# Loading order, DMA queues and weight conversion of the first batch in an FFT-mixing and MLP kernel

## Chip, cores, metric

One core of one Trainium2 chip. The metric is the device time of one execution in microseconds (us), as the median of several runs.

## The reference

```python
# x (8, 3008, 256) f32; filt_r, filt_i (1505, 256) f32
# w_in (256, 2048), w_out (2048, 256), both float64
X = np.fft.rfft(x, axis=1)
y = np.fft.irfft(X * (filt_r + 1j * filt_i)[None], n=3008, axis=1).astype(np.float32)
t = y.reshape(8 * 3008, 256)
h = t @ w_in
out = ((h * np.clip(h + 3.0, 0.0, 6.0) / 6.0) @ w_out).astype(np.float32)
```

## The kernel before

A transform of length 3008 = 47 x 64 is done as two stages of matmuls. The first goes over 64 points (`a_unit`, products `psf<-xc,wa`), the second over 47 (`b_unit`), then come the products with the filter on VectorE, the way back (`bi_unit`) and a last stage (`n_unit`, `psn`) that leaves the tokens as the MLP takes them. Between the stages the data goes through DRAM: `z_tmp` (stored by `z_store`, loaded as `t` by `t2_load`) and `g_tmp` (`g_store`, `t4_load`). While the MLP works on batch b, the transform of batch b + 1 is woven into its slots, so only batch 0 has its way to the MLP in the open. The MLP's first product is `psh`.

The weights come as float64 bits (`bits`) and are rounded to float32 on chip, in 16 pieces (`w_conv`). The filter tiles `ft` hold each frequency row twice: rows k2 + 64 s in ascending order and rows 64 j - k2 in descending order. The second kind is the "mirrored" load: 23 partitions, each fetching eight 1 KB rows backwards.

```python
def f_load(c):
    t = ft[c]
    nc.vector.memset(t, 0.0)
    lo = 1 if c == 0 else 0
    for src, p0 in ((filt_r, 0), (filt_i, HALF)):
        nc.gpsimd.dma_start(t[p0:p0 + H, :, :]..., raw(src, c * KC, [[64 * D, H], [1, KC * D]]))   # H = 24
        nc.gpsimd.dma_start(t[p0 + 32:p0 + 32 + H - 1, lo:KC, :],                                   # mirrored
                            raw(src, 64 - c * KC - lo, [[64 * D, H - 1], [-D, KC - lo], [1, D]]))
        # [cut: for c == 0 also row 32 + 64 s]

def b_unit(b, i):
    # [cut: two matmuls into ps from wb and t2]
    nc.vector.tensor_tensor(out=s1, in0=ps, in1=f, op=ALU.mult)
    nc.vector.tensor_tensor(out=s2[0:HALF], in0=ps[0:HALF], in1=f[HALF:P], op=ALU.mult)
    nc.vector.tensor_tensor(out=s2[HALF:P], in0=ps[HALF:P], in1=f[0:HALF], op=ALU.mult)

def up(b, m, jt):
    # [cut: psh = w_in x xn on TensorE]
    r = rp.tile([P, 512], FP32, name="r", tag="r")      # rp: 2 buffers
    g = gp.tile([P, 512], FP32, name="g", tag="g")      # gp: 4 buffers, shared with w_conv's temporaries
    # [cut: r = relu(psh / 6 + 0.5) on ScalarE, g = min(r, 1) * psh on VectorE]

# start of the program
nc.sync.dma_start(wa, wa_d)
for c in range(3): x_load(0, c)                  # SP's queue
for c in range(4): f_load(c)                     # GpSimd's queue
w_load(0); w_load(1)                             # GpSimd's queue
for c in range(6):
    a_unit(0, 2 * c); a_unit(0, 2 * c + 1)
    z_store(0, c)                                # GpSimd's queue
    w_conv(c); w_load(c + 2)
    # [cut: next x_load, or table_load on SP's queue]
# [cut: t2 loads, last tables]
for i in range(17):
    if i < 16:
        b_unit(0, i)
        w_conv(6 + i); w_load(8 + i)             # those past the 16th do nothing
        # [cut: t2 load]
    if i:
        bi_unit(0, i - 1)
        # [cut: g_store after every second unit, GpSimd's queue]
# [cut: t4 loads, n_unit; then the MLP with the next batch in its slots]
```

## Time and profile before

| | before |
|---|---|
| device time, median of 3 | 3359.38 us (3359.05 to 3360.88) |
| span of the profiled execution | 3356.7 us |
| second stage of batch 0 starts | 114.7 us |
| first `psh` (MLP begins) | 237.1 us |
| from first `psh` to the end | 3119.6 us, TensorE full up to its last matmul, 11.9 us before the end |

### The profile page before, as it was taken

To read this page: it belongs to the slowest core of one execution; us is meant where nothing else is said; L and a number is where in the kernel's file an instruction comes from. 1 tells how busy PE (TensorE), PEld (TensorE's weight loads), DVE (VectorE), ACT (ScalarE), POOL (GpSimd) and SP (SyncE) were. 2 spreads that over 40 slices of the span, in tenths; PEclk is the share of its full clock that TensorE was granted. 3 is DMA by queue.
4 is the path that set the end of the run, shared out by engine and by line. 5 is a ranking of instruction groups with operands and counts; after the bars stand their busy time and mean duration, and the time that the engine had idled before them with its cause. 6 is when DMAs were issued, how large, how long until landed. Compare 5 with 4: busy or idle time off the path is not lost.

```text
span 3356.7 us, 28371 instructions
## 1 busy us (share of the span) xinstructions
PE 3203.8 (95%) x11712; PEld 2117.0 (63%) x11712; DVE 919.8 (27%) x1413; ACT 740.8 (22%) x1137; POOL 218.2 (6%) x390
## 2 busy tenths in 40 slices
PE   1469999999999999999999999999999999999998
PEld 0246666666666676666675666666666666666665
DVE  2951232113321233112331133212332123311211
ACT  0012222222222222222222222222222222222221
POOL 2101000010001000010000100000000100000000
PEclk6579999999999999999999999999999999999999
DMA  8432121121212211021211212111111211010000
GB/s 149 140 100 77 32 60 39 37 58 47 55 29 62 52 45 44 24 74 47 65 28 44 62 37 63 32 55 46 52 44 29 74 43 43 24 36 19 19 7 12
DMA packets 76352, 168.20 MB, mean 50 GB/s; under 512 B 17410, under 2 KB 42244, under 8 KB 76032
## 3 DMA queue, kind: packets, MB, share of 16 engines
q0 software_dynamic: 32416, 86.55, 9.7%
q1 hardware_dynamic: 43808, 79.85, 9.2%
q8 instruction: 92, 1.51, 0.2%
q14 instruction: 36, 0.29, 0.0%
HBM read 91.29 MB, written 74.97 MB: 50 GB/s over the span
## 4 chain that ended last, share of the span: by engine, by line
PE 93%; DVE 3%; DMA 2%; issue 1%; POOL 0%; ACT 0%; SPq 0%; POOLq 0%; ACTq 0%
PE po L329 40%; PE psh L312 39%; PE psf L275 6%; PE psf L258 3%; PE psn L300 3%; PE psf L236 2%; DMA ft<-in_filt_i_dram 1%; DMA ft<-in_filt_r_dram 1%; DMA bits<-in_moe_w_in_dram 0%; DVE s L266 0%; DVE s L264 0%; DVE s L265 0%; DVE rest L213 0%; DVE rest L216 0%; DVE big L210 0%
## 5 line engine op out<-in xcount | busy, mean ns | idle before, releaser
L329 PE MATMUL po<-w_out,g 128*128 128x256 f32 (+1 forms) x6144 | 1471.9, 380 | 0.0
L312 PE MATMUL psh<-xn,w_in 128*128 128x512 f32 (+1 forms) x3072 | 1428.5, 587 | 0.0
L329 PEld LDWEIGHTS po<-w_out,g 128*128 128x128 f32 (+1 forms) x6144 | 1138.8, 188 | 398.9 <-issue 271.9
L317 DVE SCALAR_TENSOR_TENSOR g<-r,psh 128x512 f32<-128x512 f32 (+1 forms) x768 | 519.5, 676 | 2301.1 <-ACT r L316 2301.1
L316 ACT ACTIVATE r<-psh,half_c 128x512 f32<-128x512 f32 (+1 forms) x768 | 520.8, 678 | 2210.8 <-PE psh L312 2210.8
L312 PEld LDWEIGHTS psh<-xn,w_in 128*128 128x128 f32 x3072 | 573.8, 190 | 433.7 <-issue 399.2
L275 PE MATMUL psf<-s,wi 128*96 128x256 f32 x1024 | 261.6, 401 | 28.6 <-DVE s L266 28.1
L275 PEld LDWEIGHTS psf<-s,wi 128*96 128x96 f32 x1024 | 174.7, 173 | 131.9 <-issue 49.5
L236 PE MATMUL psf<-xc,wa 128*128 128x512 f32 x192 | 105.3, 639 | 76.2 <-ACT t L237 69.8
L258 PE MATMUL psf<-t,wb 96*128 96x256 f32 x512 | 139.3, 396 | 27.6 <-issue 19.0
L258 PEld LDWEIGHTS psf<-t,wb 96*128 96x128 f32 x512 | 98.5, 197 | 92.7 <-issue 67.5
L345 POOL DMA_DIRECT2D out_dram<-o x96 | 50.9, 535 | 1483.6 <-issue 1443.8
L300 PEld LDWEIGHTS psn<-wai,t 128*128 128x128 f32 x768 | 102.0, 194 | 52.6 <-issue 52.6
L280 ACT ACTIVATE t<-psf 96x512 f32<-96x512 f32 x128 | 75.9, 593 | 235.0 <-PE psf L275 235.0
L247 POOL DMA_DIRECT2D z_tmp<-t x192 | 93.4, 493 | 441.0 <-ACT t L237 414.9
L283 POOL DMA_DIRECT2D g_tmp<-t x64 | 44.6, 698 | 1069.6 <-ACT t L280 1068.6
L236 PEld LDWEIGHTS psf<-xc,wa 128*128 128x128 f32 x192 | 36.8, 203 | 117.8 <-ACT t L237 77.9
L300 PE MATMUL psn<-wai,t 128*128 128x128 f32 x768 | 102.6, 277 | 8.7 <-DMA t<-g_tmp 8.7
L264 DVE TENSOR_TENSOR s<-psf,ft 128x512 f32<-128x512 f32 x128 | 87.7, 685 | 15.2 <-PE psf L258 15.0
L266 DVE TENSOR_TENSOR s<-psf,ft 64x512 f32<-64x512 f32 x128 | 88.9, 695 | 1.8
L265 DVE TENSOR_TENSOR s<-psf,ft 64x512 f32<-64x512 f32 x128 | 87.4, 683 | 3.3
L237 ACT ACTIVATE t<-psf 128x512 f32<-128x512 f32 x96 | 56.9, 597 | 106.4 <-DMA z_tmp<-t 81.4
(34 smaller groups left out, 267.6 us busy)
## 6 DMA issues: line engine op xcount, KB each, us to landing
z_tmp<-t POOLq DMA_DIRECT2D x192, 128.0 KB, 3.6
t<-z_tmp SPq DMA_DIRECT2D x64, 384.0 KB, 3.9
g_tmp<-t POOLq DMA_DIRECT2D x64, 384.0 KB, 3.4
t<-g_tmp SPq DMA_DIRECT2D x192, 128.0 KB, 4.0
xc<-in_x_dram SPq DMA_DIRECT2D x88, 256.0 KB, 4.9
out_dram<-o POOLq DMA_DIRECT2D x88, 256.0 KB, 3.1
bits<-in_moe_w_in_dram POOLq DMA_DIRECT2D x8, 512.0 KB, 4.3
bits<-in_moe_w_out_dram POOLq DMA_DIRECT2D x8, 512.0 KB, 5.2
```

What stands on the lines that cost most here:

```text
L236: nc.tensor.matmul(ps, wa, st["x", b, c][:, 2 * r:2 * r + 2, :], start=True, stop=True)
L247: nc.gpsimd.dma_start(z_d[b, :, r0:r0 + XC, :], t[p0:p0 + 32, :, :])
L258: nc.tensor.matmul(ps[:, u, :], wb[k // KC][:, k % KC, :], st["t2", b, k // TC][:, k % TC, :], start=True, stop=True)
L264: nc.vector.tensor_tensor(out=s1, in0=ps, in1=f, op=ALU.mult)
L265: nc.vector.tensor_tensor(out=s2[0:HALF], in0=ps[0:HALF], in1=f[HALF:P], op=ALU.mult)
L266: nc.vector.tensor_tensor(out=s2[HALF:P], in0=ps[HALF:P], in1=f[0:HALF], op=ALU.mult)
L275: nc.tensor.matmul(ps[0:KR, u, :], wi[k // KC][:, k % KC, q, :], ss[q][:, u, :], start=(q == 0), stop=(q == 1))
L300: nc.tensor.matmul(ps[:, ts(q, P)], st["t4", b, m][:, q, ts(dh, P)], wai, start=True, stop=True)
L312: nc.tensor.matmul(ps[:, 0:w], w_in[:, dt, ts(jt, P)], xn[:, dt, 0:w], start=(dt == 0), stop=(dt == 1))
L316: nc.scalar.activation(out=r[:, 0:w], in_=ps[:, 0:w], func=AXT.Relu, bias=half_c, scale=1.0 / 6.0)
L317: nc.vector.scalar_tensor_tensor(out=g[:, 0:w], in0=r[:, 0:w], scalar=1.0, in1=ps[:, 0:w], op0=ALU.min, op1=ALU.mult)
L329: nc.tensor.matmul(po[q // 2][0:n, q % 2, :], g[:, ds(q * P, n)], w_out[:, jt, :], start=(jt == 0 and q % 2 == 0), stop=(jt == JT - 1 and ...
```

## The change

Its intent: x first; z stores and g stores of batch 0 on ScalarE's queue; filters and tables on SP's queue in the order in which the second stage uses them; t2 loads and weights on GpSimd's queue. The weight conversion falls from twelve VectorE instructions to nine and one multiply on GpSimd, with temporaries in a pool of their own (`cv`); a piece of `w_in` is now 256 columns of both its halves instead of 512 of one. Three conversions lie in the first stage, eight in the second (one for every second unit), and five move into the first five slots of the MLP.

```diff
+    cv = pool("cv", 4)
 def f_load(c):
-        nc.vector.memset(t, 0.0)                       # now once at the start
-            nc.gpsimd.dma_start(...)                   # ascending and mirrored
+            nc.sync.dma_start(...)
 def w_conv(i):
-        e, big, man, sgn = (gp.tile([P, 512], I32, name=n, tag="g") for n in ("e", "big", "man", "sgn"))
-        rest = rp.tile([P, 512], I32, name="rest", tag="r")
-        # [cut: 6 tensor_scalar, 3 scalar_tensor_tensor, 3 tensor_tensor on VectorE]
+        big = cv.tile([P, 512], I32, name="big", tag="cv")
+        rest = cv.tile([P, 512], I32, name="rest", tag="cv")
+        # [cut: 6 tensor_scalar, 1 tensor_tensor, 2 scalar_tensor_tensor on VectorE]
+        nc.gpsimd.tensor_tensor(out=w_part(i)[1], in0=two(rest), in1=two(hi.bitcast(FP32)), op=ALU.mult)
 # start of the program
-        for c in range(4): f_load(c)
         w_load(0); w_load(1)
         for c in range(6):
             # a_unit x 2
-            z_store(0, c)
-            w_conv(c); w_load(c + 2)
+            z_store(0, c, nc.scalar)
+            # next x_load
+            if c % 2: convert(1)                       # w_conv and the next w_load
+        for c in range(4):
+            f_load(c); table_load(c)                   # SP's queue
-        for c in range(3): t2_load(0, c)
+        for c in range(3): t2_load(0, c, nc.gpsimd)
         for i in range(17):
             # b_unit(0, i)
-                w_conv(6 + i); w_load(8 + i)
+                if i % 2 == 0: convert(1)
             # bi_unit(0, i - 1)
-                    g_store(0, i // 2 - 1)
+                    g_store(0, i // 2 - 1, nc.scalar)
+        for i in range(NCONV - done):                  # 5 are left
+            at(i, convert, 1)                          # slots 0 to 4 of the MLP
```

More of the change, by code (lines that the diff above doesn't have):

```diff
@@ L154, in f_load @@
         t = ft[c]
-        nc.vector.memset(t, 0.0)
         lo = 1 if c == 0 else 0
         for src, p0 in ((filt_r, 0), (filt_i, HALF)):
-            nc.gpsimd.dma_start(t[p0:p0 + H, :, :].rearrange("p a d -> p (a d)"),
+            nc.sync.dma_start(t[p0:p0 + H, :, :].rearrange("p a d -> p (a d)"),
                                 raw(src, c * KC, [[64 * D, H], [1, KC * D]]))
-            nc.gpsimd.dma_start(t[p0 + 32:p0 + 32 + H - 1, lo:KC, :],
+            nc.sync.dma_start(t[p0 + 32:p0 + 32 + H - 1, lo:KC, :],
                                 raw(src, 64 - c * KC - lo, [[64 * D, H - 1], [-D, KC - lo], [1, D]]))
             if c == 0:
-                nc.gpsimd.dma_start(t[p0 + 32:p0 + 32 + H, 0, :], raw(src, 32, [[64 * D, H], [1, D]]))
+                nc.sync.dma_start(t[p0 + 32:p0 + 32 + H, 0, :], raw(src, 32, [[64 * D, H], [1, D]]))
     def table_load(c):
@@ L174, in w_part @@
     def w_part(i):
+        p = i // 2
         if i % 2 == 0:
-            i //= 2
-            cols, dt = ts(i // 2, 512), i % 2
-            return moe_w_in[ts(dt, P), cols].bitcast(I32), w_in[:, dt, cols]
-        i //= 2
-        rows = moe_w_out[ts(i, 2 * P), :].bitcast(I32)
-        return rows.rearrange("(a p) d -> p a d", p=P), w_out[:, ts(i, 2), :].rearrange("p a d -> p (a d)")
+            cols = ts(p, 256)
+            src = moe_w_in[:, cols].bitcast(I32)
+            return src.rearrange("(a p) d -> p a d", p=P), w_in[:, :, cols]
+        src = moe_w_out[ts(p, 2 * P), :].bitcast(I32)
+        return src.rearrange("(a p) d -> p a d", p=P), w_out[:, ts(p, 2), :]
     def w_load(i):
@@ L186, in w_load @@
         t = op.tile([P, 1024], I32, name="bits", tag="o")
-        src = w_part(i)[0]
-        nc.gpsimd.dma_start(t if i % 2 == 0 else t.rearrange("p (a d) -> p a d", a=2), src)
+        nc.gpsimd.dma_start(t.rearrange("p (a d) -> p a d", a=2), w_part(i)[0])
         st["bits", i] = t
@@ L195, in w_conv @@
         lo, hi = words[:, :, 0], words[:, :, 1]
-        e, big, man, sgn = (gp.tile([P, 512], I32, name=n, tag="g") for n in ("e", "big", "man", "sgn"))
-        rest = rp.tile([P, 512], I32, name="rest", tag="r")
+        big = cv.tile([P, 512], I32, name="big", tag="cv")
+        rest = cv.tile([P, 512], I32, name="rest", tag="cv")
         v = nc.vector
-        v.tensor_scalar(out=e, in0=hi, scalar1=20, scalar2=0x7FF,
-                        op0=ALU.logical_shift_right, op1=ALU.bitwise_and)
@@ L201, in w_conv @@
-        v.tensor_scalar(out=e, in0=e, scalar1=1151.0, scalar2=896.0, op0=ALU.min, op1=ALU.subtract)
-        v.tensor_scalar(out=big, in0=e, scalar1=0.0, scalar2=None, op0=ALU.max)
-        v.tensor_scalar(out=e, in0=e, scalar1=20.0, scalar2=0.0, op0=ALU.subtract, op1=ALU.max)
-        v.tensor_scalar(out=man, in0=hi, scalar1=0xFFFFF, scalar2=3,
-                        op0=ALU.bitwise_and, op1=ALU.logical_shift_left)
-        v.tensor_scalar(out=sgn, in0=hi, scalar1=31, scalar2=31,
-                        op0=ALU.logical_shift_right, op1=ALU.logical_shift_left)
@@ L208, in w_conv @@
-        v.scalar_tensor_tensor(out=big, in0=big, scalar=23, in1=man,
-                               op0=ALU.logical_shift_left, op1=ALU.bitwise_or)
-        v.tensor_tensor(out=big, in0=big, in1=sgn, op=ALU.bitwise_or)
-        v.scalar_tensor_tensor(out=e, in0=e, scalar=23, in1=sgn,
-                               op0=ALU.logical_shift_left, op1=ALU.bitwise_or)
-        v.scalar_tensor_tensor(out=rest, in0=lo, scalar=9, in1=e,
-                               op0=ALU.logical_shift_right, op1=ALU.bitwise_or)
@@ L215, in w_conv @@
-        rest = rest.bitcast(FP32)
-        v.tensor_tensor(out=rest, in0=rest, in1=e.bitcast(FP32), op=ALU.subtract)
-        v.tensor_tensor(out=w_part(i)[1], in0=big.bitcast(FP32), in1=rest, op=ALU.add)
+        v.tensor_scalar(out=big, in0=hi, scalar1=3, scalar2=0x3FFFFFFF,
+                        op0=ALU.logical_shift_left, op1=ALU.bitwise_and)
+        v.tensor_scalar(out=rest, in0=hi, scalar1=30, scalar2=30,
+                        op0=ALU.logical_shift_right, op1=ALU.logical_shift_left)
@@ new lines, in w_conv @@
+        v.tensor_tensor(out=big, in0=rest, in1=big, op=ALU.bitwise_or)
+        v.tensor_scalar(out=hi, in0=hi, scalar1=20, scalar2=0x7FF,
+                        op0=ALU.logical_shift_right, op1=ALU.bitwise_and)
+        v.tensor_scalar(out=hi.bitcast(FP32), in0=hi, scalar1=897.0, scalar2=None, op0=ALU.is_ge)
+        v.tensor_scalar(out=rest, in0=big, scalar1=23, scalar2=23,
+                        op0=ALU.logical_shift_right, op1=ALU.logical_shift_left)
+        v.tensor_scalar(out=lo, in0=lo, scalar1=9, scalar2=0x3F800000,
+                        op0=ALU.logical_shift_right, op1=ALU.bitwise_or)
@@ L220, in x_load @@
+        rest, big = rest.bitcast(FP32), big.bitcast(FP32)
+        v.scalar_tensor_tensor(out=rest, in0=lo.bitcast(FP32), scalar=1.0, in1=rest,
+                               op0=ALU.subtract, op1=ALU.mult)
+        v.scalar_tensor_tensor(out=rest, in0=rest, scalar=2.0 ** -20, in1=big, op0=ALU.mult, op1=ALU.add)
+        two = lambda t: t.rearrange("p (a d) -> p a d", a=2)
+        nc.gpsimd.tensor_tensor(out=w_part(i)[1], in0=two(rest), in1=two(hi.bitcast(FP32)), op=ALU.mult)
     def x_load(b, c):
@@ L239, in a_unit, with z_store @@
             st.pop(("x", b, c))
-    def z_store(b, c):
+    def z_store(b, c, q=None):
+        q = q or nc.gpsimd
         t = st.pop(("t1", b, c))
@@ L246, in z_store, with t2_load @@
                 r0 = ri * SL + h * H + c * XC
-                nc.gpsimd.dma_start(z_d[b, :, r0:r0 + XC, :], t[p0:p0 + 32, :, :])
-    def t2_load(b, c):
+                q.dma_start(z_d[b, :, r0:r0 + XC, :], t[p0:p0 + 32, :, :])
+    def t2_load(b, c, q=None):
+        q = q or nc.sync
         t = t2p.tile([KR, TC, D], FP32, name="t2")
-        nc.sync.dma_start(t, z_d[b, ts(c, TC), :, :].rearrange("k p d -> p k d"))
+        q.dma_start(t, z_d[b, ts(c, TC), :, :].rearrange("k p d -> p k d"))
         st["t2", b, c] = t
@@ L280, in bi_unit, with g_store @@
         nc.scalar.activation(out=st["t3", b, c][:, r:r + 2, :], in_=ps[0:KR], func=AXT.Copy)
-    def g_store(b, c):
-        nc.gpsimd.dma_start(g_d[b, ts(c, TC), :, :].rearrange("k p d -> p k d"), st.pop(("t3", b, c)))
+    def g_store(b, c, q=None):
+        q = q or nc.gpsimd
+        q.dma_start(g_d[b, ts(c, TC), :, :].rearrange("k p d -> p k d"), st.pop(("t3", b, c)))
     def t4_load(b, m):
@@ L357, with convert @@
             x_load(0, c)
-        for c in range(K2 // KC):
-            f_load(c)
         w_load(0)
         w_load(1)
+        for c in range(K2 // KC):
+            nc.vector.memset(ft[c], 0.0)
+        done = 0
+        def convert(n):
+            nonlocal done
+            for _ in range(n):
+                w_conv(done)
+                w_load(done + 2)
+                done += 1
         for c in range(NB):
@@ L364 @@
             a_unit(0, 2 * c + 1)
-            z_store(0, c)
-            w_conv(c)
-            w_load(c + 2)
+            z_store(0, c, nc.scalar)
             if c + 3 < NB:
                 x_load(0, c + 3)
-            else:
-                table_load(c - 3)
+            if c % 2:
+                convert(1)
+        for c in range(K2 // KC):
+            f_load(c)
+            table_load(c)
+        nc.sync.dma_start(wai, wai_d)
         for c in range(3):
-            t2_load(0, c)
-        table_load(3)
-        nc.sync.dma_start(wai, wai_d)
+            t2_load(0, c, nc.gpsimd)
         for i in range(K2 // 2 + 1):
@@ L378 @@
                 b_unit(0, i)
-                w_conv(NB + i)
-                w_load(NB + i + 2)
                 if i % 2 and i // 2 + 3 < K2 // TC:
-                    t2_load(0, i // 2 + 3)
+                    t2_load(0, i // 2 + 3, nc.gpsimd)
+                if i % 2 == 0:
+                    convert(1)
             if i:
```

## The prediction

> **What bounds the kernel now.** The page comes first: where in the span is TensorE not full? One digit is a fortieth, 84 us.
>
> ```profile
> PE   1469999999999999999999999999999999999998
> DVE  2951232113321233112331133212332123311211
> DMA  8432121121212211021211212111111211010000
> ```
>
> TensorE is full from the fourth slice on, so only the first 240 us or so have time to give. The view by 20 us windows (columns: PE, PEld, DVE, ACT, POOL busy, TensorE's granted clock, DMA share, GB/s) splits them:
>
> ```profile
> 20.00:40.00 20.00, 0.00 (x0) 0.00 (x0) 0.00 (x0) 0.00 (x0) 3.82 (x3) 0.50 1.07 213
> 60.00:80.00 20.00, 3.64 (x4) 1.18 (x4) 6.65 (x13) 1.08 (x2) 3.46 (x7) 0.51 0.49 104
> 120.00:140.00 20.00, 13.09 (x31) 7.36 (x29) 19.30 (x36) 1.19 (x2) 1.25 (x2) 0.59 0.44 132
> 240.00:260.00 20.00, 20.00 (x70) 12.30 (x69) 4.35 (x7) 6.10 (x10) 1.98 (x4) 1.00 0.25 69
> ```
>
> Nothing computes from 20 to 40 us while the DMA engines are full; VectorE is the full one from 120 us; from 240 us it is TensorE. The chain that ended last (start, length, what) names the owners:
>
> ```profile
> 4.02 25.56 DMA ft<-in_filt_r_dram
> 29.86 26.00 DMA ft<-in_filt_i_dram
> ...
> 57.99 15.09 DMA bits<-in_moe_w_in_dram
> ...
> 225.97 3.41 DMA g_tmp<-t
> 230.72 2.84 DMA t<-g_tmp
> 233.76 3.47 PE psn L300 x16
> 237.24 1.81 PE psh L312 x4
> ```
>
> Filters and weights go ahead of the first z stores in GpSimd's queue; ScalarE, the first stage's eviction, therefore sits still (waits, us in total, times, longest):
>
> ```profile
> ACT t L237 <- DMA z_tmp<-t: 81.4, 4, 62.6
> ```
>
> The second stage (16 units of batch 0) starts at 114.7. VectorE's timeline shows what paces it:
>
> ```profile
> 118.18 0.69 DVE L266 TENSOR_TENSOR s<-psf,ft 64x512 f32<-64x512 f32 x1
> 118.90 0.43 DVE L199 TENSOR_SCALAR e<-bits 128x512 int32<-128x512 int32 x1
> ...
> 124.80 0.69 DVE L217 TENSOR_TENSOR w_in<-big,rest 128x512 f32<-128x512 f32 x1
> 125.50 0.69 DVE L264 TENSOR_TENSOR s<-psf,ft 128x512 f32<-128x512 f32 x1
> ```
>
> From one unit's first multiply to the next is 8.72 us (116.78 to 125.50): 2.1 us of products and 6.6 us for the twelve instructions of one conversion. Ten units carry a conversion (16, less the 6 of the first stage); the other six run at 3.36 us (L264 at 214.13 and 217.49). The MLP proper begins at 237.1 (first psh) and then needs 3356.7 - 237.1 = 3119.6 us of full TensorE, which the change barely touches. So the question is: when does the first psh come?
>
> **What the Trainium skill says.** (1) "DMA: Bandwidth & Descriptors", section "Why a DMA increments its semaphore by 16 and not by 1": a transfer is split over the largest k up to 16 that divides the slowest dimension of both sides; 127 partitions give 1. Half the filter loads have 23 rows (the mirrored, descending ones), a prime: k = 1, and on SP's and ScalarE's queues it is always the lowest-numbered engine. The trace agrees for k = 1: among the single packet records the mirrored loads are 356 packets of 4 KB, the first load's beginning one when the last has ended, about 182 ns apart when undisturbed, never more than three running for long. So today, from GpSimd's queue, up to three loads run beside each other on different engines. (2) "GPSIMD Engine Reference", 3.1: a two-input tensor_tensor costs about 2.6 cycles per element. From the page I estimate 512 x 2.6 / 1.2 GHz = 1.1 us for the multiply that goes there; no run here shows it yet. (3) "SBUF — State Buffer", "Who interferes with whom": a VectorE instruction with at most one SBUF input does not contend with GpSimd. The products (PSUM and ft) are such; they follow each conversion, so the multiply hides beside them.
>
> **The change part by part.**
>
> *First stage.* x is first on SP, z stores go to ScalarE's queue. First matmul at about 5 to 6 us (6.22 now). Each of 6 chunks costs ScalarE two evictions of 0.60 us and four DMA issues of about 0.45 us (SP's issues now: three in 1.37 us), 3.0 us, and waits for the landing of the z store two chunks back (4.0 us to landing). That gives 3.3 us a chunk: acts at about 7, 12, 16, 19, 22.6, 26, last issue at 29, landed near 34. Now this is after 110.
>
> *Filters and tables.* They now follow z: the built order shows the first ft loads waiting for completion lanes that the last z stores used last. From 34 us SP's queue sends per filter chunk c two 8 KB-row loads (24 rows: 12 engines), two mirrored loads (k = 1) and the two tables. Engine 0 then carries, in KB: mirrored 2 x 161 + 6 x 184 = 1426; its shares of the rest, 4 x (32 + 24 + 48) + 4 = 420. Beside it from the other queues: t2 8 x 24, g stores 5 x 24, weights 6 x 32 = 504. At 48 ns per KB for the mirrored ones (the 1 KB packets of t<-z_tmp take 46 ns and follow each other at 46 to 50) and 182 / 4 = 45.5 for the rest: 68 + 42 = 110 us. All filters and tables are there at F = 34 + 110 = 144. The chunks come at about 59, 86, 115 and 144.
>
> *Second stage.* Conversion: six tensor_scalar (0.34 when independent, 0.46 when the next one reads the result, as in today's spacing), one tensor_tensor and two scalar_tensor_tensor at about 0.72: 4.5 us in place of 6.6, and 8 of them instead of 10. Alone that would make a pair of units 2 x 2.1 + 4.5 = 8.7 us of VectorE, at best 9.7 with TensorE's turns, so 16 units take 78 us. But four units need 28 us of filter transfer against 19 of work: VectorE is not the bound, engine 0 is. Also, g stores sit in ScalarE's queue and share eight completion lanes with SP: the built order has the second g store waiting for the lane of a mirrored load of chunk 2, the fourth for one of chunk 3. Evictions behind it stop. This keeps units 8 to 11 back, yet not beyond F. After F come units 12 to 15: 1 us for the first matmul, 4 x 2.1 + 2 x 4.5 = 17.4 on VectorE, about 4 for the last product and eviction: last eviction F + 22.5. From the last eviction (225.1) to the first psh it is 12 us now; the way (store, load, psn) stays. First psh: 144 + 34.5 = 178.5, a gain of 58.6.
>
> *First MLP block.* Five conversions move into slots 0 to 4. VectorE then needs 4.5 + 0.7 = 5.2 us a slot against about 3.9 of TensorE (1.72 + 1.73, and 0.86 for a first-stage unit in every second slot), 6.6 us over five slots. Psh has two buffers and the down product lags by two slots, which takes up some; the GpSimd multiply blocks the next conversion's start for about half a microsecond. Loss: 5 us.
>
> Sum: 3359.4 - 58.6 + 5 = 3305.8. Engine 0 may overlap packets of two rings (the 1.07 above is a sum of packet times over 1), so a little less: 3303.
>
> **The rivals.**
> - *The mirrored loads do not pile up on one engine from SP* (spread, or rotating as today). Then chunk 0 is there near 50, VectorE and TensorE pace 78 us, last eviction at about 130, first psh at 142: gain 95 - 5, time 3269. Against it: k = 1 shows in today's packets and the instruction is the same; for it: every HWDGE transfer in this trace divides by 16, so none shows the lowest-engine rule.
> - *Engine 0 is slower than I take it.* Today's mirrored packets take 250 to 400 ns under the tables' traffic, though that includes the wait for other packets that I count separately. At 60 ns per KB for the mirrored ones F becomes 34 + 86 + 42 = 162, the time by the same sum 3324.
> - *Filters are hidden anyway, conversion was the bound* (the change's own intent): the first rival's 3269, since the new VectorE work is what remains.
> - *The MLP's first block loses more*: if VectorE sets all five slots and GpSimd blocks it fully, 10 us instead of 5: 3308.
>
> **Range and chances.** Four in five for the one-engine story, 3303 give or take 12; one in five for about 3270. Faster by over 2% means below 3292.2. That gives 0.31 faster, 0.68 within 2%, 0.01 slower; range 3267 to 3325.
>
> **What would show it.** Mirrored ft loads landing one after the other, 8 to 14 us apart, until about 144; second-stage units in four groups with idle TensorE and VectorE between; ScalarE waiting long with a g store in its queue; the first psh near 178; VectorE full over the first 25 us of the MLP. Wrong would be: units at an even 9 to 10 us a pair from 50 us on with VectorE full (first rival), a first stage that ends after 45, or POOL multiplies well over 1.1 us that VectorE waits for.

## The result

3308.51 us (3308.25 to 3309.39, four runs) against 3359.22 us (3357.64 to 3360.88). The ratio is 0.9849, with a 95% interval of 0.9835 to 0.9863: 1.5% less time, within the 2% that was given 0.68, and 5.5 us from the 3303 on record. Ratios here are the mean time of one kernel's fast runs over that of the other's of the same rounds, so not quite the ratio of the medians quoted.

**Where the time came from.** The strips of the page after the change, a fortieth (83 us) per digit:

```profile
PE   3589999999999999999999999999999999999998
DVE  4642332123311332113321233212332123312211
DMA  6442110211112121121211112122110211010000
```

TensorE is near full from the third slice on instead of the fourth. The chain of waits that ended last, start, length and what, gives the story of batch 0:

```profile
30.93 17.79 DMA ft<-in_filt_i_dram
...
53.03 4.73 DMA z_tmp<-t
58.05 8.43 DMA t<-z_tmp
66.58 2.06 PE psf L260 x4
71.66 27.35 DMA ft<-in_filt_r_dram
100.16 2.09 PE psf L260 x4
106.69 16.08 SPq L158
123.11 21.22 DMA wb<-wb_t
144.47 2.06 PE psf L260 x4
...
178.36 2.62 PE psh L315 x4
```

The second stage does not wait for VectorE any more. It waits for filters and tables, again and again: 27 us for a filter load, 16 us in SP's sequencer (SPq), 21 us for a table behind the filters. The 27 us reach the stage by a detour: not a product but ScalarE's g store at 99.09 waits for that load, whose completion semaphore it needs (see below), and the evictions wait behind the store. The last group of units is released at 144.47. The first psh comes at 178.36, 58.9 us sooner than the 237.24 of before.

The windows of 20 us (columns as in the prediction) show that nothing computing is full there:

```profile
40.00:60.00 20.00, 3.58 (x4) 1.18 (x4) 0.00 (x0) 1.75 (x4) 1.95 (x3) 0.59 0.55 157
80.00:100.00 20.00, 9.56 (x39) 6.36 (x37) 14.25 (x26) 2.27 (x4) 5.45 (x6) 0.84 0.56 157
120.00:140.00 20.00, 10.62 (x36) 7.32 (x34) 13.41 (x25) 2.15 (x4) 3.92 (x4) 0.74 0.46 125
```

VectorE had 19.30 of 20 us from 120 to 140 before; now it has 13.41. And the DMA engines as a whole are only about half busy (0.46 to 0.56): transfers are the limit, but not their total. The packet records say which: the mirrored loads' 1 KB packets on SP's queue form eight runs that never overlap, 8.9 to 15.5 us each, about 98 us together, from 25 to 143 us. In the least disturbed run the packets are 48 ns apart on average. From 66 to 70 us hardly anything else is in flight, and the DMA engines move 24 GB/s at a mean share of 0.07, close to one engine of sixteen (0.0625). The records don't name the engine; that it is the same one for all eight runs is inferred from their never overlapping.

**What the prediction did not have.** ScalarE's own timeline, with its queue (ACTq: issue of a store) and the wait ahead of each eviction in brackets:

```profile
26.13 13.27 ACTq L248 DMA_DIRECT2D z_tmp<-t  x4
39.58 1.09 ACT L237 ACTIVATE t<-psf 128x512 f32<-128x512 f32 x2 [13.48 <-DMA ft<-in_filt_r_dram]
40.70 9.26 ACTq L248 DMA_DIRECT2D z_tmp<-t  x4
```

The filters did not follow z. SP issued the first at 21.86, before the fourth to sixth z stores, and those stores then waited behind filter loads: the program hands a small set of completion semaphores to the transfers of both queues in turn, and a store whose semaphore a mirrored load still holds can't be issued (the one at 38.62 waited for the semaphore of the first mirrored load, whose last packet ended at 38.22). z was there at about 58 us instead of 34.

SP's queue shows a second thing, one issue each (start, length):

```profile
71.66 0.25 SPq L160 DMA_DIRECT2D ft<-in_filt_r_dram  x1
71.96 18.39 SPq L158 DMA_DIRECT2D ft<-in_filt_i_dram  x1
...
90.88 14.55 SPq L166 DMA_DIRECT2D wb<-wb_t  x1
```

The issue of a mirrored load (L160) takes 0.25 us, but the issue after it takes 14.55 or 18.39 us. No wait for a semaphore is recorded inside these. All eight issues that follow a mirrored load are long, 3.97 to 18.39 us each; an ordinary one takes 0.25 to 0.45 us. So a mirrored load holds up not only its engine but also the whole queue behind it. No run takes these two apart: where the engine's backlog goes, the long issues go too (from the first filter load to 140 us none is over 0.7 us in e1, and 1.54 is the longest in e2).

**Where some was given back.** VectorE in the MLP's second slot, one slot from `g` to `g`:

```profile
186.66 0.68 DVE L320 SCALAR_TENSOR_TENSOR g<-r,psh 128x512 f32<-128x512 f32 x1
187.25 1.14 DVE L200 TENSOR_SCALAR big<-bits 128x512 int32<-128x512 int32 x1
188.32 0.41 DVE L202 TENSOR_SCALAR rest<-bits 128x512 int32<-128x512 int32 x1
...
192.30 0.68 DVE L320 SCALAR_TENSOR_TENSOR g<-r,psh 128x512 f32<-128x512 f32 x1
```

A slot takes 5.64 us (192.30 - 186.66) while VectorE converts. TensorE is idle for 5.0 us in the stretch from 188 to 238. From the first psh to the end of the last matmul it is 3107.76 us before and 3114.61 after: 6.9 us more. 5.0 of it is this idle time, 0.9 is a granted clock of 0.91 instead of 1.00 in the first 10 us, and 1.0 is not accounted for. After the last matmul the span goes on for 13.7 us instead of 11.9. The spans balance: 58.9 - 6.9 - 1.8 = 50.2 = 3356.7 - 3306.5.

### The profile page after: what moved, and what is told of

Its sections match the earlier page's. It is cut to its first block, busy times and chain, and to the rows that moved or that the text cites. A ratio compares the mean times of both kernels' runs of the same rounds, so it can differ in the third digit from the quotient of the medians.

```text
span 3306.5 us, 28366 instructions
## 1 busy us (share of the span) xinstructions
PE 3190.7 (96%) x11712; PEld 2112.7 (64%) x11712; DVE 890.0 (27%) x1365; ACT 742.0 (22%) x1137; POOL 210.9 (6%) x364
## 4 chain that ended last, share of the span: by engine, by line
PE 94%; DMA 3%; DVE 2%; SPq 1%; issue 0%; ACT 0%; ACTq 0%; POOLq 0%; POOL 0%
PE po L332 40%; PE psh L315 39%; PE psf L277 6%; PE psf L260 3%; PE psn L303 3%; PE psf L236 2%; DMA ft<-in_filt_r_dram 1%; DMA wb<-wb_t 1%; DMA ft<-in_filt_i_dram 1%; SPq L158 1%; DMA xc<-in_x_dram 0%; DMA z_tmp<-t 0%; DMA t<-z_tmp 0%; DVE big L200 0%; SPq L163 0%; DVE big L204 0%
## 5 line engine op out<-in xcount | busy, mean ns | idle before, releaser
L277 PE MATMUL psf<-s,wi 128*96 128x256 f32 x1024 | 252.6, 391 | 6.2 <-DVE s L268 3.4
L248 POOL DMA_DIRECT2D z_tmp<-t x168 | 82.1, 496 | 399.5 <-ACT t L237 396.7
```

What stands on the lines that cost most here:

```text
L248: q.dma_start(z_d[b, :, r0:r0 + XC, :], t[p0:p0 + 32, :, :])
L277: nc.tensor.matmul(ps[0:KR, u, :], wi[k // KC][:, k % KC, q, :], ss[q][:, u, :], start=(q == 0), stop=(q == 1))
```

## The experiments

Ten kernels ran; each is an edit of the changed kernel unless said otherwise. Three rounds each, beside the kernel before (3359.2 to 3359.4 us).

| kernel | us, median | ratio to before, 95% interval | 2nd stage starts | first psh | end of last matmul to end of span |
|---|---|---|---|---|---|
| before | 3359.2 | 1 | 114.7 | 237.1 | 11.9 |
| changed | 3308.5 | 0.9849 [0.9835, 0.9863] | 66.6 | 178.2 | 13.7 |
| e1_spread | 3280.2 | 0.9761 [0.9747, 0.9776] | 57.9 | 150.9 | 13.7 |
| e2_mirror_pool | 3298.0 | 0.9817 [0.98, 0.9833] | 85.4 | 172.2 | 8.5 |
| e3_old_conv | 3345.4 | 0.9959 [0.9944, 0.9974] | 66.9 | 182.9 | 13.7 |
| e4_conv_only | 3336.9 | 0.9933 [0.9918, 0.9948] | 111.8 | 213.7 | 13.0 |
| e6_spaced | 3302.0 | 0.9828 [0.9814, 0.9843] | 67.2 | 178.3 | 13.7 |
| e7_spread_spaced | 3272.4 | 0.9746 [0.9731, 0.976] | 56.3 | 146.7 | 13.7 |
| e8_spread_spaced_pool | 3270.7 | 0.9735 [0.9719, 0.9752] | 66.4 | 153.3 | 8.3 |
| e9_g_pool | 3267.0 | 0.9729 [0.9714, 0.9744] | 59.9 | 149.8 | 7.5 |
| e10_pool_stores | 3302.4 | 0.983 [0.9815, 0.9844] | 56.8 | 178.3 | 8.5 |
| e11_z_pool | 3265.8 | 0.9723 [0.9707, 0.974] | 64.9 | 150.1 | 6.6 |

The last three columns come from one profiled execution of each kernel. How far they repeat shows in e1 and e7, which have the same program up to the MLP: the first psh comes at 150.9 in one and at 146.7 in the other. Differences of up to 4 us at the first psh between the kernels with cut loads are therefore not read as effects below.

The theory: mirrored loads of 23 rows run on one engine and set the second stage's pace. The rivals: the tables' bytes do it, or the conversion, or ScalarE's stores waiting for completion semaphores.

**e1_spread.** The same bytes, but 16 of the 23 mirrored rows go in a load that can use 16 engines.

```diff
-            nc.sync.dma_start(t[p0 + 32:p0 + 32 + H - 1, lo:KC, :],
-                              raw(src, 64 - c * KC - lo, [[64 * D, H - 1], [-D, KC - lo], [1, D]]))
+            for r0, nr in ((0, 16), (16, H - 1 - 16)):
+                nc.sync.dma_start(t[p0 + 32 + r0:p0 + 32 + r0 + nr, lo:KC, :],
+                                  raw(src, 64 * (r0 + 1) - c * KC - lo, [[64 * D, nr], [-D, KC - lo], [1, D]]))
```

> The changed kernel, with each mirrored filter load of 23 rows cut into one of 16 and one of 7 rows, so that none of them runs on one DMA engine alone; same bytes, same 1 KB packets, same queue. One-engine theory: filters and tables no longer set the second stage; VectorE and TensorE do, about 9.7 us a pair of units, first psh near 142 in place of 178, time about 3272 (3262 to 3282). Rival 1, the filters are slow for their packet size, their row pitch or the total bandwidth: within 8 us of the changed kernel's 3308. Rival 2, the conversions on VectorE already set the pace: within 5 us of 3308.

3280.17 us, as the one-engine theory had it; the time the others named is not met. Its windows:

```profile
20.00:40.00 20.00, 7.50 (x12) 2.52 (x12) 7.67 (x14) 4.24 (x8) 4.13 (x4) 0.82 0.97 304
60.00:80.00 20.00, 16.61 (x46) 10.18 (x46) 19.37 (x35) 1.78 (x3) 5.44 (x6) 0.67 0.49 135
80.00:100.00 20.00, 9.51 (x39) 6.24 (x37) 14.23 (x26) 2.05 (x4) 5.44 (x6) 0.84 1.05 248
```

From 20 to 40 us the DMA engines move 304 GB/s at a share of 0.97, where the changed kernel had 195 at 0.63. VectorE is full from 60 to 80. But the stage has a hole of 11 us from 89 to 100. SP issues the tables of chunk 2 only at 75.29; from 80 to 100 us the DMA engines are full (1.05), and the g store issued at 81.59 takes 17.75 us to land. ScalarE's next eviction waits for that landing, since the tile it writes (`t3`) has two buffers and the store still reads one. So the first psh comes at 150.9, not at the 142 that an even pace would give.

**e2_mirror_pool.** The uncut mirrored loads from GpSimd's queue, where before had them.

```diff
-            nc.sync.dma_start(t[p0 + 32:p0 + 32 + H - 1, lo:KC, :],
+            nc.gpsimd.dma_start(t[p0 + 32:p0 + 32 + H - 1, lo:KC, :],
```

> The changed kernel, with the uncut 23-row loads issued from GpSimd's queue as in the kernel before; everything else as changed. Each load still runs on one engine, but in the kernel before they ran up to three side by side. If the pile-up of all eight on the same engine is the cost: filters done earlier by 25 to 50 us, time 3270 to 3290. If one engine a load is enough of a cost by itself (the eight loads take as long as now): 3300 to 3312. GpSimd's queue is also in order with the t2 loads, which may give back some 5 us.

3298.02 us: between the two, a miss for both. The pile-up itself is confirmed. Several of the same 23-row loads are in flight at once: issued from 30.12 to 70.22 us, they have all landed by 84.2, where in the changed kernel the last packet ends at 142.7. Once the stage runs it has no holes (VectorE 19.33 of 20 us from 100 to 120). But the t2 loads now stand behind the mirrored ones in GpSimd's queue:

```profile
70.22 1.63 POOL L160 DMA_DIRECT2D ft<-in_filt_i_dram  x1
71.84 2.05 POOL L253 DMA_DIRECT2D t<-z_tmp  x3
```

The chain of waits:

```profile
39.70 45.67 issue
85.36 2.06 PE psf L260 x4
```

The second stage starts at 85.4 instead of 66.6. The expectation had this wait at some 5 us; it is 19, and costs most of what the spreading earns. The first psh is 6.0 us sooner than in the changed kernel; the other 5.2 us of its lead lie after the last matmul (8.5 instead of 13.7 us).

**e10_pool_stores.** Batch 0's z and g stores on GpSimd's queue, the filters as changed. It takes ScalarE out of the shared set of semaphores, and leaves the mirrored loads alone.

```diff
-            z_store(0, c, nc.scalar)
+            z_store(0, c)
-                    g_store(0, i // 2 - 1, nc.scalar)
+                    g_store(0, i // 2 - 1)
```

> The changed kernel, with batch 0's z and g stores back on GpSimd's queue, so that ScalarE issues none and they share no completion lane with the filter loads. One-engine theory: engine 0 has the same work, from about 22 us on, so filters and tables are there at 135 to 144 as now; time 3298 to 3310. Rival 3, the queue and lane sharing (ScalarE stuck behind filter loads with its stores) costs the second stage its time: second stage earlier by 20 us or more, time below 3290.

3302.36 us. The stage starts 10 us sooner, yet the first psh is the same (178.3). The chain of waits:

```profile
56.77 2.06 PE psf L260 x4
74.04 17.20 SPq L158
91.58 12.65 SPq L166
105.50 15.43 SPq L158
121.27 22.41 DMA wb<-wb_t
143.82 2.06 PE psf L260 x4
```

The last group is released at 143.82 (144.47 in the changed kernel), and SP's long issues are still there without any store on ScalarE. ScalarE's waits are a consequence, not the bound. Of the 6 us by which this kernel is faster, 5.2 lie after the last matmul (8.5 instead of 13.7 us), and none in batch 0.

**e3_old_conv.** The twelve-instruction conversion of before in the changed kernel, with its temporaries in `gp` and `rp`.

```diff
-        # short conversion, temporaries in cv, last multiply on GpSimd
+        # the conversion of the kernel before, temporaries in gp and rp, all on VectorE
```

> The changed kernel with the twelve-instruction conversion of the kernel before (all on VectorE, 6.6 us in place of 4.5), everything else as changed. One-engine theory: until the last filter chunk VectorE waits anyway, so of the eight conversions in the second stage only the two after it lie on the path, 2 x 2.1 = 4 us; the five of the first MLP block cost a slot of 7.3 us in place of the 5.64 measured, about 8 us: time 3318 to 3324. Rival 2, VectorE's conversions pace the second stage: 8 x 2.1 = 17 us there and the same 8: 3330 to 3338.

3345.36 us, a miss. The first psh moves by only 4.8 us (182.9), so in the changed kernel the conversion's length hardly matters to the second stage; the one-engine theory had said 4. The rest, 32 us, is lost in the MLP. The waits of TensorE's first MLP product on VectorE (us in total, times, longest), here and then in the changed kernel:

```profile
PE psh L316 <- DVE g L321: 26.1, 5, 5.2
```

```profile
PE psh L315 <- DVE g L320: 4.9, 3, 2.0
```

With the old conversion each of the five slots takes 10.6 to 12.7 us. The longer waits are 21 us of the 32; beside them TensorE's granted clock is only 0.83 over the 90 us from 192.9, where it stays at 1.00 from 188 on in the changed kernel. The old conversion's temporaries take turns in the same four buffers as `g` and the same two as `r`, so a slot can't overlap with the next. The changed kernel has a pool of its own for them, and slots of 5.64 us. What of the 26 us is due to the pool and what to the longer conversion, this run can't tell.

**e4_conv_only.** The other half: the kernel before with the short conversion and the `cv` pool, queues as they were.

```diff
-        # conversion of before
+        # w_part, w_load and w_conv of the changed kernel, cv = pool("cv", 4)
```

> The kernel before with the short conversion alone (its tiles, its slices of the weights and the GpSimd multiply with it), order and queues as before. In the kernel before, ten conversions stand in the second stage, which VectorE paces at 8.72 us a unit: 10 x 2.1 = 21 us, and in the first stage from 73 to 110 us a chunk waits for a conversion of 6.6 us: up to 10 more. Time 3328 to 3340. If the conversion is hidden there too: over 3350.

3336.9 us, as expected; the first psh is 23.3 us sooner than before. In the kernel before VectorE paces the stage, so a shorter conversion pays there. In the changed kernel it would not (e3). The two halves don't add up: everything but the short conversion (queues, order, and five conversions moved into the MLP) brings 54.1 us to the first psh (e3), the short conversion alone 23.3, both together 58.9.

**e6_spaced.** The five conversions of the MLP in every second slot.

```diff
-            at(i, convert, 1)
+            at(2 * i, convert, 1)
```

> The changed kernel, with the five conversions of the first MLP block in slots 0, 2, 4, 6, 8 in place of 0 to 4. From first psh to end it takes 3306.5 - 178.2 = 3128.3 us in the changed kernel's profile and 3119.6 in the kernel before: 8.7 us that I put down to VectorE overfull by one conversion a slot. If so, VectorE has 7.8 us a two slots for 4.5 + 1.4 of work, and 6 to 9 us come back: 3300 to 3303. If the 8.7 us come from something else (transfers of batch 1, the GpSimd multiply holding VectorE up): less than 3 us come back.

3302.0 us, as expected; TensorE's idle time in the first block falls from 5.0 to 0.26 us with the first psh unmoved.

**e7_spread_spaced.** e1 and e6 together.

> Mirrored loads cut in 16 and 7 rows, and the five conversions of the first MLP block in every second slot. If the two are independent, the 28 us of the first and the 6.5 us of the second add up: 3272 to 3276.

3272.42 us: the two add up within the spread of the runs (28.3 and 6.5 us would give 3273.7).

**e8_spread_spaced_pool, e9_g_pool, e11_z_pool.** The stop in e1's stage was put down to g stores on ScalarE's queue that hold up SP's next loads. e8 puts z and g stores of e7 on GpSimd's queue, e9 only the g stores, e11 only the z stores.

```diff
# e8: both lines; e9: the second; e11: the first
-            z_store(0, c, nc.scalar)
+            z_store(0, c)
-                    g_store(0, i // 2 - 1, nc.scalar)
+                    g_store(0, i // 2 - 1)
```

> The same, with batch 0's z and g stores on GpSimd's queue. With the loads cut, the second stage still has a hole of 10 us near 90 us in which ScalarE and SP's table load wait for each other's completion lanes (g stores and tables share them), and the mirrored-on-GpSimd run showed 75 us for 16 units without such a hole against 81. If the hole is due to the shared lanes, it goes: 3258 to 3268. If the hole is the tables' own transfer: no more than 3 us off the run before it.

> The spread and spaced kernel (3272.4), with batch 0's g stores on GpSimd's queue and the z stores left on ScalarE's. If the stop of the second stage comes from g stores that share completion lanes with SP's filter and table loads: it starts at about 56 as in that kernel, has no hole, and the first psh comes at 142 to 144; the time is 3266 to 3269 from that, and 3261 to 3264 if the shorter end after the last matmul (8.3 instead of 13.7 us) comes with the g stores. If moving the stores from ScalarE's queue gains nothing here but the shorter end: 3267 and a first psh of 147. If it is 3272 or more, the lanes cost nothing and neither does the end.

> The opposite half: z stores of batch 0 on GpSimd's queue, g stores on ScalarE's. If the later start of the second stage in the kernel with both on GpSimd (66 instead of 56) comes from the z stores: it starts at about 66 here too, the first psh comes at 153 or later, and the time is 3276 to 3282, or 3271 to 3277 if the shorter end comes with the z stores. If the start was late by chance or by the g stores: start at 56 and 3272.

3270.66, 3267.0 and 3265.84 us. TensorE's first product of the second stage in e9 and in e11:

```profile
59.88 3.75 PE L261 MATMUL psf<-t,wb 96*128 96x256 f32 x8 [25.80 <-DMA t<-z_tmp]
```

```profile
64.91 3.75 PE L261 MATMUL psf<-t,wb 96*128 96x256 f32 x8 [26.31 <-DMA ft<-in_filt_i_dram]
```

With the z stores on GpSimd the stage starts later (64.9 and 66.4 against 56.3 and 59.9), as expected. It then takes less time, from its first product to psn 81.7 and 83.3 us against 86.9 (e7) and 86.4 (e9). For the first psh this comes out even at best: none of the three is earlier than e7, with all stores on ScalarE (146.7). So the shared semaphores do make waits (in e11 SP waits 23.8 us for one g store) but taking the stores away buys nothing for batch 0 that these runs show. The wait for a `t3` buffer also stays without shared semaphores: in e9 ScalarE still stands 5.7 us for a g store to land (6.6 in e7). The expectations for e8 and e9 that rested on this (a first psh of 142 to 144 in e9) fall, and so does e11's of 3271 or more.

e9's other branch (3267, a first psh of 147, nothing gained but the shorter end) fits its time. e9 and e11 owe their lead over e7 to the end of the program: 7.5 and 6.6 us after the last matmul instead of 13.7. e8 has the shorter end too (8.3), but a first psh 6.5 us later, and is not faster than e7 by more than the noise. This shorter end shows in every kernel of the table in which some of batch 0's stores or mirrored loads went back to GpSimd's queue, and in none of the other variants of the changed kernel. The trace shows where it lies: after its last DMA issue GpSimd runs one drain instruction (in the trace's records, though the timeline view leaves it out), and the other engines wait for it. That drain takes 11.17 us in the changed kernel, where SP is done 7 us before it ends, and 3.93 us in e11; across the kernels it differs as the end does. Why it differs stays open: the kernel before has all of these on GpSimd and a drain of 9.36 us.

e11 and e9 are the fastest, 2.8% and 2.7% under before, and apart by less than their intervals.

## Why the prediction was right, point by point

- **One engine carries the mirrored loads, and this is the bound: right.** Eight loads in series, the stage in groups with TensorE and VectorE idle between, VectorE below 15 of 20 us (five groups, where four were forecast). e1 and e10 confirm it from both sides: spread the loads and the first psh comes 27 us sooner, free the stores and it doesn't move.
- **The filters are all there at 144: right in the sum, wrong in its terms.** The prediction took a start of 34 and 110 us. The start failed at "They now follow z": the first issue came at 21.86 and the first mirrored packets at 25. The duration failed at "68 us" for the mirrored part: about 98 us measured, 69 ns per KB with what interleaves (98 over 1426 KB) instead of 48. Where other queues' packets take turns with the mirrored ones, a run is longer (15.5 us at most against 8.9), so counting all of them apart at full speed understated it; for these runs the second rival's 60 ns was nearer. Against that, only some 19 us lie between the runs, where "42" was taken for everything else. In all it is 117 us from 25 to 143, and the last table behind them lands at 144.3. A start 9 us too late and a length 7 us too short nearly cancelled; that the 144 came out to the microsecond is luck.
- **First stage ends at 34: wrong.** z landed at about 58 us, so that one of the prediction's own signs of being wrong ("a first stage that ends after 45") did come true. This is because the stores waited behind mirrored loads for completion semaphores. The prediction had seen this coupling for g stores and not for z stores. It cost nothing in the end, as e10 shows: a start at 56.8 gives the same 143.8.
- **The chunks at 59, 86, 115, 144:** TensorE was released at 66.6, 100.2, 115.3, 130.1 and 144.5. The first is 8 us late for z; the last fits.
- **From the last release to the first psh, 34.5: right,** 178.36 - 144.47 = 33.9. The conversion was taken as 4.5 us and took 4.44 (70.79 to 75.23), a pair of units 8.70 against 8.7.
- **The first MLP block loses 5: right** (5.0 idle), and e6 shows it by taking it away. The mechanism was only half seen. The prediction used the skill's "SBUF — State Buffer", section "Who interferes with whom", for the products, and left out the condition that stands there, "outside the 2-port perf modes". The same section lists tensor_scalar among those that can use both ports and then contend with GpSimd, whoever issues first blocking the other. In the MLP slots the conversion's first tensor_scalar follows just after the GpSimd multiply has begun, and takes 1.13 to 1.14 us instead of 0.43: 0.7 us a slot. The trace fits the section; no run moves the multiply to test it.
- **The total:** 3359.4 - 58.6 + 5 = 3305.8 against 3308.5. Of what is missing, the longer end is 1.8 us and the lower clock in the first 10 us 0.9; another 1.0 us of the MLP is not accounted for, and against these stand 0.3 us more gained at the first psh and some 0.7 us between the spans and the device times. The further 2.8 us that the prediction took off for overlapping packets are nowhere in the trace; without them it would have been nearer.
- **The rivals.** That the loads don't pile up: false. Its 3269 was also not what spreading gives: e1 has 3280, since the stage starts at 58 instead of 50 and has holes. That the conversion is the bound: true before (e4), false after (e3). That the MLP block loses 10: false.

## What to carry to other kernels

Before moving loads to another queue, look at the row count of each. By the rule of the Trainium skill that the prediction cites ("DMA: Bandwidth & Descriptors", "Why a DMA increments its semaphore by 16 and not by 1"), 23 rows, which no number from 2 to 16 divides, go to one engine, and from SP or ScalarE always to the same. No run shows the engine's number, but here such loads did run one behind the other and held up the issuing queue as well. Cut such a load into a part that divides by 16 and a rest: that one line was worth 28 us here, more than half of what the whole change earned. A change that removes one bound earns only up to the next one, so shares of the gain measured alone (54 and 23) don't add, and a short piece of work that is moved into a full pipeline is better put in every second slot than in each (6.5 us here).

## What the Trainium skill lacked or had wrong

- "DMA: Bandwidth & Descriptors", "Issuing engines are not separate DMA queues", says that issuing from several engines at once only saves sequencer time, "usually small relative to the DMA itself". It lacks that the issue behind a one-engine load can itself be long: 3.97 to 18.39 us on SP against 0.25 to 0.45 normally, here a part of the path that sets the end. The rule for the number of engines in its section "Why a DMA increments its semaphore by 16 and not by 1" fits: eight 23-row loads ran in series, at a share of about one engine in sixteen.
- "GPSIMD Engine Reference", 3.1: the 1.1 us worked out from its per-element figure for a multiply of 512 elements was 1.27 to 1.28 us measured (one of them 1.39); the 0.17 us between them is some 200 cycles at its 1.2 GHz. The page names what comes on top (the broadcast, the call, for which it has "tens of cycles", and the join of the eight cores) but gives no sum for it.
- "Runtime: NRT & Kernel Launch", "The ~15µs preamble/postamble breakdown", gives fixed parts for what follows a kernel. It lacks that the end can differ between kernels of the same tail: 6.6 to 13.7 us here between the last matmul and the end of the span, of which GpSimd's drain is 3.93 to 11.17 us. e7 and e11 (13.7 and 6.6) differ only in the queue that z stores took 3 ms earlier. No run shows what of this is the page's postamble.
